# An attention and top-8 feed-forward kernel: the work after the last attention block rebuilt

## The chip, the cores and the metric

The kernel runs on one core of a Trainium2 chip. TensorE (PE) multiplies matrices, ScalarE (ACT) applies functions, VectorE (DVE) and GpSimd (POOL) work element by element, and SyncE (SP) issues the DMAs. The metric is the device time of one execution in microseconds; lower is better.

## What is computed

x is 2048 tokens by 448 features. With LN for a layer norm without weights:

```
h  = x + MHA(LN(x))        # 16 heads of 28, one shared K and V, softmax over all 2048 tokens
n  = LN(h)
r  = n @ w_r               # one score per token
idx = the 8 tokens with the largest r
y  = (silu(n[idx] @ w_gate) * (n[idx] @ w_up)) @ w_down * sigmoid(r[idx])
out = h + n, and y added to the 8 rows idx
```

w_gate and w_up are 448 x 1792, w_down is 1792 x 448. So 2040 of the 2048 rows of the output are known as soon as h is; only eight wait for the feed-forward part.

## The kernel before

**Blocks.** After a head that normalises x (16 tiles of 128 tokens) and makes K, V and Q, the attention runs as 16 blocks. Block b takes four heads (g = b % 4) and 512 queries (b // 4). For each of 16 key tiles PE makes scores into PSUM (`qk`, L593), either ACT turns 1024 of them into weights with Exp (`act_unit`, L601) or DVE does it with integer arithmetic (`dve_unit` L614, three `shift` L620), and PE multiplies with V into an accumulator bank, 6 or 7 (`act_pv`, `dve_pv`). Each block's accumulator holds four heads; one row per head is the row sum of the softmax.

**Row sums.** `post_block` (L499) copies the accumulator to SBUF (Ot, L506; on ACT for block 15), and then sends the row sums through DRAM: Ot's four sum rows to a scratch (L509), the scratch spread over 128 partitions into Lc (L510), DVE takes minimum and maximum for a flag and the reciprocal (L511 to L515), Lc goes back to the scratch (L516), and one row is read by 32 partitions each into Rb (L517). POOL multiplies Ot by Rb into On (L518). After every fourth block `out_proj` (L524) projects the four On for each of four token tiles, adds x, takes the layer norm's statistics, and writes outf (h + n, in place of x), xn (n) and the router score r (a weighted sum, L567, and a correction, L570). For blocks 3, 7 and 11 this runs beside the next block; for block 15 nothing runs beside it.

**After block 15.** The scores of all 16 tiles are transposed by PE, copied, sent by a DMA into one row of 2048 (L716), and DVE finds the eight largest and their places (L718, L719). A dozen small DVE steps split places and weights into bf16 parts, PE spreads them over the partitions (L736, L739), DVE makes a one-hot matrix oh (L743) and its transpose ohT (L746). PE gathers the eight rows of xn by 64 matmuls with oh (L749), then runs gate and up (56 matmuls each, L756), ACT and DVE form silu(g) * u * weight (L758 to L765), and 14 matmuls of 448 columns give y (L768). Then PE adds y into all 16 output tiles (L777: ohT as the stationary operand, and the identity times outf for every second tile), ACT or DVE copies each to ofin, and four DMAs of 448 KB store the output (L788).

**Order.** Nothing of this is scheduled by a compiler. Every step is recorded with a planned duration and a priority (`G.op`), and `plan` (L79) walks through a simulated time and gives each engine a fixed order: at each moment the ready step of lowest priority goes, and where only steps of a high priority are ready, they go early. Priorities are 16 per block: `at(16 * b + ...)`. At run time every engine follows its list strictly and waits on semaphores. So a step whose input comes later than planned holds all that stands behind it on its engine.

A second program in the kernel recomputes everything in a safer way if the flag says that a row sum left its range; it isn't run on these inputs.

## Time and profile before

| | |
|---|---|
| three runs | 473.23 us median (472.95 to 475.53) |
| the profiled execution | 475.65 us, its span 473.9 us |
| mean granted clock of TensorE | 0.924 |
| busy in the span | PE 365.2 us, PE weight loads 111.1, DVE 372.3, ACT 385.8, POOL 47.1 |
| instructions | 7880 |

The span runs from the first to the last instruction of the profiled execution. ACT is busy for 81% of it, but not evenly: it is nearly full until the last block ends at about 407 us, and then mostly idle.

### The profile page before, as it was taken

To read this page: it belongs to the slowest core of one execution; us is meant where nothing else is said; L and a number is where in the kernel's file an instruction comes from. 1 tells how busy PE (TensorE), PEld (TensorE's weight loads), DVE (VectorE), ACT (ScalarE), POOL (GpSimd) and SP (SyncE) were. 2 spreads that over 40 slices of the span, in tenths; PEclk is the share of its full clock that TensorE was granted. 3 is DMA by queue.
4 is the path that set the end of the run, shared out by engine and by line. 5 is a ranking of instruction groups with operands and counts; after the bars stand their busy time and mean duration, and the time that the engine had idled before them with its cause. 6 is when DMAs were issued, how large, how long until landed. Compare 5 with 4: busy or idle time off the path is not lost.

```text
span 473.9 us, 7880 instructions
## 1 busy us (share of the span) xinstructions
PE 365.2 (77%) x3228; PEld 111.1 (23%) x3228; DVE 372.3 (79%) x783; ACT 385.8 (81%) x430; POOL 47.1 (10%) x65
## 2 busy tenths in 40 slices
PE   1888798988879889888798888887988887240685
PEld 1333122222222222222222222221222222010630
DVE  5899469998968998999799899995898995046332
ACT  1488699999989999999899999997999999314012
POOL 8010001011011111010101010101020101310000
PEclk9988799999999999999999999998999999766565
DMA  8950000000000000000000000000000000000004
GB/s 220 254 163 10 0 25 3 24 3 25 2 24 1 23 4 26 3 24 1 24 3 24 3 24 3 23 5 24 1 25 3 23 3 24 3 21 1 1 8 154
DMA packets 15938, 14.62 MB, mean 31 GB/s; under 512 B 5960, under 2 KB 12888, under 8 KB 15896
## 3 DMA queue, kind: packets, MB, share of 16 engines
q1 hardware_dynamic: 15896, 14.05, 10.5%
q8 instruction: 27, 0.44, 0.4%
q14 instruction: 15, 0.12, 0.1%
HBM read 11.94 MB, written 2.10 MB: 30 GB/s over the span
## 4 chain that ended last, share of the span: by engine, by line
ACT 41%; DVE 24%; PE 22%; DMA 7%; issue 3%; POOL 2%; SPq 0%; POOLq 0%; DVEq 0%
ACT P L601 40%; PE ps L341 22%; DVE Y L614 8%; DVE Y L620 6%; DMA Rb<-l_scr 3%; DMA x_sb<-in_A_x_dram 1%; DVE Ot L506 1%; POOL On L518 1%; DVE K L481 1%; DVE bn L440 1%; DMA l_scr<-Lc 1%; DVE xnT L469 1%; DVE Vs L492 1%; PE ps L344 1%; DVE xn L455 1%
## 5 line engine op out<-in xcount | busy, mean ns | idle before, releaser
L601 ACT ACTIVATE P<-ps 128x1024 bf16<-128x1024 f32 x398 | 370.0, 1094 | 20.5 <-PE ps L341 19.1
L341 PE MATMUL ps<-Q,K 64*128 64x512 bf16 x1024 | 186.6, 391 | 48.4 <-ACT P L601 31.2
L614 DVE TENSOR_SCALAR Y<-ps 128x512 int16<-128x512 f32 x228 | 146.9, 681 | 21.5 <-PE ps L341 21.1
L620 DVE TENSOR_SCALAR Y<-Y 128x2048 int16<-128x2048 int16 x171 | 118.4, 731 | 1.6
L341 PEld LDWEIGHTS ps<-Q,K 64*128 64x128 bf16 x1024 | 45.0, 93 | 196.5 <-ACT P L601 147.9
L341 PE MATMUL ps<-P,Vs 128*32 128x512 bf16 x796 | 80.6, 395 | 0.7 <-ACT P L601 0.7
L341 PE MATMUL ps<-Y,Vs 128*32 128x512 bf16 x912 | 72.2, 381 | 0.0
L518 POOL TENSOR_TENSOR On<-Ot,Rb 128x512 bf16<-128x512 f32 x16 | 22.3, 1391 | 298.9 <-DMA Rb<-l_scr 298.9
L341 PEld LDWEIGHTS ps<-P,Vs 128*32 128x32 bf16 x796 | 20.5, 93 | 53.0 <-issue 51.1
L341 PE MATMUL ps<-wo_pad,On 128*128 128x448 bf16 x64 | 17.9, 399 | 12.7 <-POOL On L518 12.7
L341 PEld LDWEIGHTS ps<-Y,Vs 128*32 128x32 bf16 x912 | 23.1, 96 | 17.0 <-issue 7.2
L341 PE MATMUL ps<-xnT,wq_pad 112*128 112x512 bf16 x64 | 21.4, 430 | 2.9 <-DVE Ot L506 2.7
L534 DVE TENSOR_TENSOR hbuf<-ps,x_sb 128x448 f32<-128x448 f32 x16 | 9.9, 621 | 15.6 <-PE ps L341 15.6
L344 PE MATMUL ps<-ident,xn 128*112 128x128 bf16 x64 | 6.8, 271 | 12.2 <-POOL vone L397 10.6
L432 DVE TENSOR_SCALAR Q<-ps,qone 128x512 bf16<-128x512 f32 x16 | 11.6, 727 | 5.7 <-PE ps L341 5.6
L782 ACT ACTIVATE xnT<-ps 128x448 bf16<-128x448 f32 x8 | 4.3, 543 | 13.0 <-PE ps L341 13.0
L511 DVE TENSOR_TENSOR Lmn<-Lmn,Lc 128x16 f32<-128x16 f32 x16 | 2.7, 169 | 14.5 <-DMA Lc<-l_scr 14.5
L506 DVE COPY Ot<-ps 128x512 f32<-128x512 f32 x15 | 10.3, 684 | 4.9 <-PE ps L341 4.7
L541 ACT ACTIVATE st<-st 128x1 f32<-128x1 f32 x4 | 0.8, 190 | 16.1 <-DVE st L538 16.1
L546 POOL TENSOR_TENSOR st<-st,nhalf 128x1 f32<-128x1 f32 x12 | 8.3, 692 | 47.5 <-DVE st L538 47.5
L440 DVE BATCH_NORM_STATS2 bn<-x_sb 128x6 f32<-128x448 bf16 x16 | 9.4, 604 | 4.4 <-DMA x_sb<-in_A_x_dram 4.4
L758 ACT ACTIVATE eg<-ps 128x112 f32<-128x112 f32 x1 | 0.3, 263 | 13.4 <-PE ps L341 13.4
(122 smaller groups left out, 190.8 us busy)
## 6 DMA issues: line engine op xcount, KB each, us to landing
Rb<-l_scr SPq DMA_DIRECT2D x16, 256.0 KB
out_dram<-xnT SPq DMA_DIRECT2D x4, 448.0 KB, 3.2
wg_sb<-in_B_w_gate_dram SPq DMA_DIRECT2D x1, 1568.0 KB, 12.7
wu_sb<-in_B_w_up_dram SPq DMA_DIRECT2D x1, 1568.0 KB, 18.5
wd_sb<-in_B_w_down_dram SPq DMA_DIRECT2D x1, 1568.0 KB, 22.2
x_sb<-in_A_x_dram SPq DMA_DIRECT2D x3, 448.0 KB, 6.5
x_sb<-in_A_x_dram SPq DMA_DIRECT2D x2, 224.0 KB, 2.8
wq_sb<-in_A_wq_dram SPq DMA_DIRECT2D x1, 392.0 KB, 5.3
```

The source lines that it names most:

```text
L341: return lambda e: e.matmul(o, lhsT=l, rhs=r, start=start, stop=stop)
L344: return lambda e: e.transpose(o, i, ident[0:p, 0:p])
L432: G.op(DV, lambda e: e.tensor_scalar(Q[:, b % 4, :], ps[:, bank, :], qone[:, 0:1], None, ALU.add), dvt(512), reads=[pk(bank), "qone"], wri ...
L440: G.op(DV, [lambda e, t=t: e.bn_stats(bn6[:, t, :], x_sb[:, t, :])], dvt(D), reads=[("x", t)], writes=[("bn6", t)])
L455: G.op(DV, lambda e, t=t: e.tensor_scalar(xn[:, t, :], x_sb[:, t, :], mv[:, t, 0:1], rstd[:, t:t + 1], ALU.subtract, ALU.mult), 340, reads ...
L506: (lambda e: e.tensor_copy(Ot[:, rb, :], ps[:, acc_bank(b), :])), dvt(512), reads=[pk(acc_bank(b))],
L518: G.op(PO, lambda e: e.tensor_tensor(On[:, qb % 2, g, :], Ot[:, rb, :], Rb[:, rb, :], ALU.mult), 1270, reads=[("Ot", rb), ("Rb", rb)], wri ...
L534: G.op(DV, lambda e: e.tensor_tensor(hbuf[:, hr, :], ps[:, bank, 0:D], x_sb[:, t, :], ALU.add), dvt(D), reads=[pk(bank), ("x", t)], writes ...
L546: G.op(PO, lambda e: e.tensor_tensor(st[:, t, 4:5], st[:, t, 7:8], nhalf[:, 0:1], ALU.pow), 570, reads=[("st7", t), "nhalf"], writes=[("st ...
L601: G.op(AC, lambda e: e.activation(P[:, sl, :, :], ps[:, b0:b0 + 2, :], ACT.Exp, bias=EBIAS, scale=OCT), 905, reads=[pk(b0), pk(b0 + 1)], w ...
L614: G.op(DV, lambda e, k=k: e.tensor_scalar(Y[:, n, 0, p + 2 * k, :].bitcast(I16), ps[:, 4 + k, :], 0.0, 32639.0 - 3 * STEP, ALU.max, ALU.mi ...
L620: G.op(DV, lambda e: e.tensor_scalar(Y[:, n, v, :, :].bitcast(I16), Y[:, n, 0, :, :].bitcast(I16), v * STEP, None, ALU.add), 610, reads=[( ...
```

## The change

Everything up to the end of block 15 keeps its arithmetic; some work is put into it, and what comes after is rebuilt.

- **Row sums of block 15** take no DRAM trip: DVE clamps the accumulator into Ot in two halves, a matmul with a 0/1 matrix `sel` in fp32 spreads each head's sum over its 32 partitions, ACT takes Exp(-Ln), and DVE multiplies the accumulator by it in four quarters. The DMAs to Lc stay, for the flag alone.
- **Last four token tiles**: three of the four projection matmuls and the addition of x (by the identity) are issued before block 15 ends (`last_pre`, 16 matmuls), one each is left (`last_proj`). Statistics are taken straight from PSUM. The router score no longer needs the 448-wide sum after the norm: two more columns of `wo_pad` hold wo @ w_r (as a high and a low part) and xw holds x @ w_r, both worked out by DVE ahead of time (`last_w`, 8 wide sums at priority 40).
- **Router in two stages**: the 12 tiles known by block 13 are ranked during block 14 (`first_top`, `first_max`), their top eight rows are fetched by two indirect DMAs from POOL during block 15 (`second_top`); at the end only 8 + 512 scores are ranked, read by DVE from PSUM.
- **Stores**: after blocks 3, 7 and 11 SP stores 512 output rows and, to a scratch, 512 rows of xn (448 KB each). The last 512 output rows go as soon as they exist.
- **Feed-forward**: the eight rows are gathered by 20 matmuls with 128 stationary columns instead of 64 with 112. silu uses ACT (Exp, Ln, Exp) instead of a reciprocal on DVE. The down projection has w_down stationary: 56 matmuls with 8 moving columns on top of 20 that bring the rows of outf; PE transposes the result, DVE copies it, and POOL writes the eight final rows by one indirect DMA, which waits for all the stores.
- x_sb's rows grow from 448 to 452 columns, wo_pad's from 448 to 450; POOL sets up some small tables in the head; x_sb, xn and wd_sb get 16 spare columns at their ends, so that a slice of 128 columns never runs out. A step of POOL that overwrites what an earlier step of POOL reads now waits for it.

The diff, cut to its core:

```diff
+        if last:
+            G.prio = u - 30
+            for h in range(2):
+                c = slice(256 * h, 256 * h + 256)
+                G.op(DV, lambda e, c=c: e.tensor_scalar(Ot[:, rb, c], ps[:, acc_bank(b), c], LO / 4, HI * 4, ALU.max,
...
+                G.op(PE, mm(ps[:, 1, c], sel[:, :], Ot[:, rb, c], True, True), 450, reads=["sel", ("OtH", h)],
+                G.op(AC, lambda e, c=c: e.activation(Rb[:, rb, c], ps[:, 1, c], ACT.Ln), 270, reads=[pk(1)],
+                G.op(AC, lambda e, c=c: e.activation(Rb[:, rb, c], Rb[:, rb, c], ACT.Exp, scale=-1.0), 270,
...
+                    G.op(DV, lambda e, q=q: e.tensor_tensor(On[:, qb % 2, g, q], ps[:, acc_bank(b), q], Rb[:, rb, q],
+                                                            ALU.mult), 200,
+                         reads=[pk(acc_bank(b)), ("RbH", h)], writes=[("OnQ", k)])
...
+        if not last:
+            G.op(DV, lambda e: e.reciprocal(Lc[:, rb, :], Lc[:, rb, :]), 200, reads=[("Lc", rb)], writes=[("Lc", rb)])
+            dma(scr[b, 1].rearrange("i (r k) -> (i r) k", k=16), Lc[:, rb, :], [("scr1", b)], reads=[("Lc", rb)])
+            dma(Rb[:, rb, :], scr[b, 1].unsqueeze(1).broadcast_to([4, 32, 512]), [("Rb", rb)], reads=[("scr1", b)])
+            G.op(PO, lambda e: e.tensor_tensor(On[:, qb % 2, g, :], Ot[:, rb, :], Rb[:, rb, :], ALU.mult), 1270,
+                 reads=[("Ot", rb), ("Rb", rb)], writes=[("On", qb % 2, g)])
...
+        if k == 3:
+            evs.append(dma(out_v[:, t - 3:t + 1, :], outf[:, t - 3:t + 1, :], [("out", qb)],
+                           reads=[("outf", i) for i in range(t - 3, t + 1)]))
+            dma(xs[(t - 3) * 128:(t + 1) * 128, :].rearrange("(n p) d -> p n d", p=128), xn[:, t - 3:t + 1, :],
+                [("xs", qb)], reads=[("xn", i) for i in range(t - 3, t + 1)])
...
+        G.op(PE, mm(ps[0:12, bank, 0:128], x_sb[:, 0:12, D + 2], ident[:, :], True, True), 200,
+        G.op(DV, lambda e: e.tensor_copy(r12[:, :], ps[0:12, bank, 0:128]), 200, reads=[pk(bank)], writes=["r12"])
+        for c in range(3):
+            dma(r_row[0:1, 512 * c:512 * c + 512].rearrange("o (t p) -> o t p", p=128), r12[4 * c:4 * c + 4, :],
+                [("r_row", c)] + (old if c == 0 else []), reads=["r12"] + (old if c else []))
...
+        G.op(DV, lambda e: e.max(top8[:, 0, :], r_row[:, :]), 1700, reads=[("r_row", c) for c in range(3)],
+        G.op(DV, lambda e: e.max_index(idx8[:, 0, :], top8[:, 0, :], r_row[:, :]), 1760,
...
+        G.op(PE, mm(ps[0:8, bank, 0:1], posf[:, 0, :], ones1[:, 0:1], True, True), 100, reads=["ones1", ("posf", 0)],
+        G.op(DV, lambda e: e.tensor_scalar(idc[:, :], ps[0:8, bank, 0:1], 0.0, 1535.0, ALU.max, ALU.min), 70, reads=[pk(bank)], writes=["idc"])
+        G.op(DV, lambda e: e.tensor_copy(extc[:, D:D + 2], idb[:, :]), 70, reads=["idb0", "idb1"] + old,
...
+        for src, dst, nm, rd in ((out[0, 0:1536, :], extc, "extc", "out"), (xs, xnc, "xnc", "xs")):
+            G.op(PO, lambda e, src=src, dst=dst: e.indirect_dma_start(
+                dst[:, 0:D], None, src, bass.IndirectOffsetOnAxis(ap=idc[:, 0:1], axis=0)), 1000, dma=True,
+                reads=["idc"] + old + [(rd, q) for q in range(3)], writes=[nm])
...
+    def last_w():
+        for g in range(4):
+            G.op(DV, lambda e, g=g: e.scalar_tensor_tensor(junk[:, :], wo_pad[:, g, 0:D], 1.0, w_rb[:, :],
+                                                           ALU.mult, ALU.mult, accum_out=wor[:, g:g + 1]), 600,
+                 reads=["wo_pad", "w_rb"], writes=["junk", ("wor", g)])
...
+            G.op(DV, lambda e, k=k: e.scalar_tensor_tensor(junk[:, :], x_sb[:, 12 + k, 0:D], 1.0, w_rb[:, :],
+                                                           ALU.mult, ALU.mult, accum_out=xw[:, k:k + 1]), 600,
...
+        fns = [mm(ps[:, bank, 0:D + 2], On[:, 1, g, k * 128:(k + 1) * 128], wo_pad[:, g, :], g == 0, False)
+               for g in range(3)] + [mm(ps[:, bank, 0:D], ident[:, :], x_sb[:, t, 0:D], False, False)]
...
+        G.op(PE, mm(ps[:, bank, 0:D + 2], On[:, 1, 3, k * 128:(k + 1) * 128], wo_pad[:, 3, :], False, True), 200,
+        G.op(DV, lambda e: e.bn_stats(bn6[:, t, :], ps[:, bank, 0:D]), dvt(D), reads=[pk(bank)], writes=[("bn6", t)])
+        G.op(DV, lambda e: e.bn_aggr(mv[:, t, :], bn6[:, t, :]), 95, reads=[("bn6", t)], writes=[("mv", t)])
+        G.op(AC, lambda e: e.activation(st[:, t, 7:8], mv[:, t, 1:2], ACT.Ln, bias=EPS), 200,
+        G.op(AC, lambda e: e.activation(st[:, t, 4:5], st[:, t, 7:8], ACT.Exp, scale=-0.5), 200,
+        G.op(DV, lambda e: e.tensor_scalar(ra[:, k, 0:1], ps[:, bank, D:D + 1], ps[:, bank, D + 1:D + 2],
+                                           xw[:, k:k + 1], ALU.add, ALU.add), 85,
...
+        G.op(AC, lambda e: e.activation(xn[:, t, :], ps[:, bank, 0:D], ACT.Identity, bias=st[:, t, 6:7],
+                                        scale=st[:, t, 4:5]), 650,
+             reads=[pk(bank), ("st4", t), ("st6", t), ("st4", 15)], writes=[("xn", t)], prio=u + 20)
...
+            G.op(AC, lambda e: e.activation(outf[:, t, :], ps[:, bank, 0:D], ACT.Identity, bias=st[:, t, 6:7],
+                                            scale=st[:, t, 5:6]), 650,
+                 reads=[pk(bank), ("st5", t), ("st6", t), ("st4", 15)], writes=[("outf", t)])
...
+            G.op(DV, lambda e: e.tensor_scalar(outf[:, t, :], ps[:, bank, 0:D], st[:, t, 5:6], st[:, t, 6:7],
+                                               ALU.mult, ALU.add), 540,
+                 reads=[pk(bank), ("st5", t), ("st6", t), "oh5"], writes=[("outf", t)])
+        if k % 2:
+            evs.append(dma(out_v[:, t - 1:t + 1, :], outf[:, t - 1:t + 1, :], [("out", 3, k)],
+                           reads=[("outf", i) for i in range(t - 1, t + 1)]))
...
+                    at(16 * b + (14.6 if k < 3 else 17.0) + 0.1 * k, last_pre, k)
+                    at(16 * b + 20.0 + k, last_proj, k)
+    at(16 * 11 + 36.0, first_top)
+    at(16 * 14 + 4.0, first_max)
+    at(16 * 15 + 2.0, second_top)
+    at(16 * 2 + 8.0, last_w)
...
+        G.op(PE, mm(ps[0:1, 3, k * 128:(k + 1) * 128], x_sb[:, 12 + k, D + 2:D + 3], ident[:, :], True, True), 100,
+    G.op(DV, lambda e: e.max(top8[:, 1, :], row), 620, reads=[pk(2), pk(3)], writes=[("top8", 1)])
+    G.op(DV, lambda e: e.max_index(idx8[:, 1, :], top8[:, 1, :], row), 700, reads=[pk(2), pk(3), ("top8", 1)],
+    G.op(PE, mm(ps[:, 1, 0:8], ones1[:, :], posf[:, 1, :], True, True), 100, reads=["ones1", ("posf", 1)],
...
+        oh5[:, :, :], iota_n[:, :].unsqueeze(2).broadcast_to([128, 5, 8]),
+        ps[:, 1, 0:8].unsqueeze(1).broadcast_to([128, 5, 8]), ALU.is_equal), 150, reads=["iota_n", pk(1)],
+        writes=["oh5"])
...
+            fns.append(mm(psg[:, ch, :], xn_raw[:, o:o + 128], oh5[:, k, :], k == 0, False))
+        fns.append(mm(psg[:, ch, :], xnc[:, ch * CK:ch * CK + 128], oh5[0:8, 4, :], False, True))
...
+            fns.append(mm(psy[:, ch, :], x_raw[:, o:o + 128], oh5[:, k, :], k == 0, False))
+        fns.append(mm(psy[:, ch, :], extc[:, ch * CK:ch * CK + 128], oh5[0:8, 4, :], False, False))
+    G.op(AC, lambda e: e.activation(eg[:, :, :], pg[:, :, :], ACT.Exp, scale=-1.0), 170, reads=[pk(2)], writes=["eg"])
+    G.op(AC, lambda e: e.activation(eg[:, :, :], eg[:, :, :], ACT.Ln, bias=1.0), 170, reads=["eg"], writes=["eg"])
+    G.op(AC, lambda e: e.activation(eg[:, :, :], eg[:, :, :], ACT.Exp, scale=-1.0), 170, reads=["eg"], writes=["eg"])
-    G.op(PE, [mm(ps[0:8, 3, 0:D], guT[:, fc, :], wd_sb[:, fc, :], fc == 0, fc == NFC - 1) for fc in range(NFC)], 4800,
-         reads=["guT", "wd_sb"], writes=[pk(3)])
-    G.op(DV, lambda e: e.tensor_copy(yp[:, :], ps[0:8, 3, 0:D]), 600, reads=[pk(3)], writes=["yp"])
-        if on_act:
-            fns.append(mm(ps[:, bk, 0:D], ident[:, :], outf[:, t, :], False, True))
-        G.op(PE, fns, 230 * len(fns), reads=["ohT", "yp", "ident", ("outf", t)], writes=[pk(bk)])
-        if on_act:
...
-            evs.append(dma(out_v[:, t - 3:t + 1, :], ofin[:, t - 3:t + 1, :], [("out", t)],
...
+    G.op(PE, [mm(psy[:, ch, :], wd_raw[:, fc * D + ch * CK:fc * D + ch * CK + 128], guT[:, fc, :], False,
+                 fc == NFC - 1) for ch in range(NCH) for fc in range(NFC)], 1500,
+    G.op(PE, [mm(ps[0:8, 2, ch * CK:(ch + 1) * CK], yT[0:CK, ch, :], ident[0:CK, 0:CK], True, True)
+              for ch in range(NCH)], 400, reads=["yT", "ident"], writes=[pk(2)])
+    G.op(DV, lambda e: e.tensor_copy(fin[:, :], ps[0:8, 2, 0:D]), dvt(D), reads=[pk(2)], writes=["fin", "wq_sb"])
+    o = G.op(PO, lambda e: e.indirect_dma_start(out[0], bass.IndirectOffsetOnAxis(ap=idxc[:, 0:1], axis=0),
+                                                fin[:, :], None), 1000, dma=True,
+             reads=["fin", "idxc"] + [("out", q) for q in range(3)] + [("out", 3, 1), ("out", 3, 3)],
```

## Rows read from the trace of the kernel before

**Rows 1.** The page's chain of work that ended last, by engine, shares of the span.

```profile
ACT 41%; DVE 24%; PE 22%; DMA 7%; issue 3%; POOL 2%; SPq 0%; POOLq 0%; DVEq 0%
```

**Rows 2.** Windows by stage: PE, PEld, DVE, ACT, POOL busy (xcount), PEclk, DMA, GB/s.

```profile
64.00:404.00 340.00, 289.13 (x2638) 78.87 (x2638) 299.16 (x580) 331.28 (x359) 29.30 (x27) 0.99 0.05 14
407.40:419.50 12.10, 0.19 (x2) 0.09 (x2) 1.16 (x9) 0.60 (x1) 3.91 (x3) 0.57 0.08 24
419.50:431.80 12.30, 4.76 (x16) 1.92 (x16) 8.91 (x36) 6.27 (x16) 0.00 (x0) 0.78 0.00 0
431.80:442.30 10.50, 0.75 (x8) 0.38 (x8) 7.99 (x20) 0.77 (x2) 0.00 (x0) 0.50 0.00 1
442.30:448.80 6.50, 6.13 (x64) 6.07 (x65) 0.19 (x1) 0.00 (x0) 0.00 (x0) 0.50 0.01 3
448.80:452.90 4.10, 3.12 (x112) 3.05 (x112) 1.89 (x5) 0.26 (x1) 0.00 (x0) 0.50 0.02 4
452.90:458.40 5.50, 4.74 (x15) 1.59 (x15) 0.61 (x1) 0.00 (x0) 0.00 (x0) 0.64 0.00 0
458.40:473.90 15.50, 9.54 (x24) 1.81 (x24) 4.90 (x8) 4.34 (x8) 0.00 (x0) 0.56 0.37 123
```

**Rows 3.** Timeline of ACT: start us, us, instruction, idle before it and its releaser.

```profile
329.69 2.10 ACT L601 ACTIVATE P<-ps 128x1024 bf16<-128x1024 f32 x2 [3.21 <-PE ps L341]
407.44 0.60 ACT L505 ACTIVATE Ot<-ps 128x512 f32<-128x512 f32 x1 [0.57 <-PE ps L341]
```

**Rows 4.** Timeline of POOL: the row-sum products of blocks 11 and 14.

```profile
325.69 1.68 POOL L518 TENSOR_TENSOR On<-Ot,Rb 128x512 bf16<-128x512 f32 x1 [21.73 <-DMA Rb<-l_scr]
398.50 1.27 POOL L518 TENSOR_TENSOR On<-Ot,Rb 128x512 bf16<-128x512 f32 x1 [21.39 <-DMA Rb<-l_scr]
```

**Rows 5.** Timeline of DVE: blocks 1 and 2, and the end of block 15.

```profile
59.96 0.69 DVE L506 COPY Ot<-ps 128x512 f32<-128x512 f32 x1 [4.74 <-PE ps L341]
71.57 2.98 DVE L620 TENSOR_SCALAR Y<-Y 128x2048 int16<-128x2048 int16 x3
...
396.12 1.90 DVE L620 TENSOR_SCALAR Y<-Y 128x2048 int16<-128x2048 int16 x3
411.33 0.17 DVE L511 TENSOR_TENSOR Lmn<-Lmn,Lc 128x16 f32<-128x16 f32 x1 [13.32 <-DMA Lc<-l_scr]
```

**Rows 6.** Timeline of PE: the fp32 matmul of the flag (one in the code).

```profile
412.31 0.19 PE L341 MATMUL ps<-ones,bad 128*1 128x1 f32 x2 [4.99 <-DVE bad L702]
```

**Rows 7.** Groups by form: out<-in shapes xcount | busy us, mean ns | idle before.

```profile
L341 PE MATMUL ps<-oh,xn 128*112 128x8 bf16 x64 | 6.1, 234 | 1.5 <-DVE oh L743 1.5
L341 PE MATMUL ps<-xselT,wg_sb 112*128 112x8 bf16 x56 | 1.6, 168 | 0.4 <-DVE xselT L752 0.4
L341 PE MATMUL ps<-wd_sb,guT 128*8 128x448 bf16 x14 | 4.7, 518 | 1.0 <-DVE guT L765 1.0
L567 DVE SCALAR_TENSOR_TENSOR junk<-hbuf,st,w_rb 128x448 bf16<-128x448 f32 x16 | 10.9, 678 | 0.0
L536 DVE BATCH_NORM_STATS2 bn<-hbuf 128x6 f32<-128x448 f32 x16 | 10.0, 624 | 0.1
L554 ACT ACTIVATE x_sb<-hbuf,st 128x448 bf16<-128x448 f32 x4 | 3.0, 756 | 1.3 <-DVE st L550 1.2
L718 DVE MAX8 top<-Y 1x8 f32<-1x2048 f32 x1 | 2.3, 2283 | 1.9 <-DMA Y<-r 1.9
L758 ACT ACTIVATE eg<-ps 128x112 f32<-128x112 f32 x1 | 0.3, 263 | 13.4 <-PE ps L341 13.4
L763 DVE TENSOR_TENSOR sg<-ps,sg 128x112 f32<-128x112 f32 x1 | 0.3, 274 | 0.0
```

**Rows 8.** Chain of waits in order of time, one small DVE step: start, us, what.

```profile
425.33 0.07 DVE st L550
```

**Rows 9.** Issue to landing, us min/median/max: the four output stores, then the row-sum DMAs.

```profile
DMA to landing us min/median/max: 2.8/3.2/4.8
...
DMA to landing us min/median/max: 1.4/1.5/2.5
```

More of the change, by code (lines that the diff above doesn't have):

```diff
@@ L574, in _main @@
+    out_v = out[0].rearrange("(n p) d -> p n d", p=128)
+    evs = []
     groups = [4] * NB
@@ L657, in _main @@
             chunk(c)
+        last_w()
         nx = 0
@@ L772, in _main @@
[L772 to L789 removed]
+    G.prio = 310
@@ L790, in _main @@
+    evs.append(o)
     G.close(evs, "flag")
```

382 lines of the change are left out of this document (222 added, 160 removed).

## The prediction

> **What bounds the kernel now.** I read the chain of waits by engine first: ACT holds 41% of it, DVE 24%, PE 22% [rows 1], so there is more than one limit. The windows by stage say where each holds. From 64 to 404 us ACT is busy for 331.28 of 340 us, at a granted clock of 0.99 [rows 2]: the attention is bound by ACT's Exp, and PE (289.13) and DVE (299.16) run beside it with some 51 and 41 us to spare, about 3 us in each of its fifteen blocks. At 407.44 ACT takes the last accumulator [rows 3], and from there 66.5 us run to the end of the span, in which no engine is full over more than one stage. This tail is a chain of single steps: row sums 12.1 us, projection and norm 12.3, router 10.5, gather 6.5, gate and up 4.1, down 5.5, output 15.5 [rows 2]. What is taken off this chain comes off the time; what is put into the attention costs only what ACT loses by it.
>
> **The tail, part by part.** Times are worked out as the length of the new chain in each stage, with 0.03 to 0.05 us for each hop between engines.
>
> Row sums: four DMAs one behind the other and POOL's product go. In their place DVE clamps 256 columns: between 0.274 us for 112 and 0.624 for 448 [rows 7] that is 0.42. PE spreads them in fp32: one fp32 matmul shows as two records [rows 6], so two passes; 448 columns take 4.7 / 14 = 0.34 us [rows 7], 256 columns twice 0.39, with the drain 0.5 (bounds: one pass 0.3, four passes 0.9). ACT takes Ln and Exp, between 0.263 at 112 columns and 0.60 at 512 [rows 3, 7] 0.38 each. DVE multiplies the first quarter, 0.29. With hops 2.15 us; the second half follows beside the projection. Saved: 9.95.
>
> Projection and norm: one matmul a tile, 0.5 with its drain. DVE then does four statistics (0.624, some 0.54 apart) and about twenty one-column steps at 0.07 [rows 7, 8], 3.6 us, and after the last statistics a chain of aggregate, Ln, Exp and score, 0.9. The adds of x, the wide router sums (0.678 each [rows 7]) and ACT's 0.756 us outputs ahead of the last tile's Ln are gone from the path. 5.05 instead of 12.3; saved 7.25 (bounds 4 and 7 us for the stage).
>
> Router: PE's transposes 0.3; the maximum of 520 scores, 2.283 x 520 / 2048 = 0.58 [rows 7] and 0.1 of fixed time, 0.69; the search the same and 0.08; a cast, a spreading matmul and a one-hot of 40 columns 0.6; 0.3 until ACT's fourth xn (4 x 0.756 after the last Exp) is there. 2.7, where 10.5 held a DMA and two searches of 2.28. Saved 7.8. The new search reads PSUM, which no row shows; if it paid the full row's price, 3.2 more.
>
> Gather: 64 matmuls with 112 stationary columns took 6.1 us, 0.096 each; 56 with 128 took 1.6, 0.029 each [rows 7]. The new 20 have 128 columns, so I take 0.029: 0.6, with drain, copy and hops 1.1. Saved 5.4 (at 0.096 it would be 4.1).
>
> Gate and up stay at 3.12; the 20 matmuls that bring outf add 0.6 behind them, and silu (three ACT steps at 0.263 and three DVE steps at 0.274 [rows 7]) fits beside up and these. 3.75 instead of 4.1; saved 0.35.
>
> Down: 56 x 0.029 = 1.65, a copy 0.2, four transposes 0.4, a copy of 448 columns 0.62, hops: 3.05 instead of 5.5. Saved 2.45 (at 0.096 each it would be 1.3 us slower than now).
>
> Output: 24 matmuls, 16 copies and four stores in 15.5 us become one store of eight rows. No row shows an indirect DMA. Below, it is a small DMA: 1.5 us [rows 9]; above, the slowest store, 4.8 [rows 9], and two POOL steps of 1.27 [rows 4] and hops to make descriptors, 8. I take 3.0, a small DMA and one POOL step, since the data are small, and 0.5 to the end. Saved 12.0. What it waits for is earlier: the last two stores leave about when the router ends, eight microseconds before. The Trainium skill, page "DMA: Bandwidth & Descriptors", section "Anatomy of one DMA — SWDGE (gpsimd) path", gives about 2.0 us as the fixed price; by that the sum would be 1 us lower.
>
> Together 45.2 us: the tail would take 21.3 instead of 66.5.
>
> **What the attention pays.** (1) `last_w` and the head. It takes eight sums of 0.678 us and more. Four, those with wo, wait for four DMAs that the planner now thinks 14 us long each; they fall into block 2, where DVE has its share of spare time. The other four, with x, are ready early and fill every gap that the planner sees while K and Q are still being made; each then delays DVE by up to its length. DVE sits idle 4.74 us ahead of 59.96 [rows 5], so not all of it counts: 0.8 for both, with POOL's dozen set-up steps (bounds 0 and 6). (2) Router, first stage: 1.7 + 1.8 us of searches, a copy and some small steps, 4.5 us on DVE in blocks 13 to 15. DVE's last work in the attention ends at 398.02 and its next starts at 411.33, after 13.32 idle [rows 5], so it can be 9 us late at the end; what counts is PE held by DVE: 0.8 (bounds 0 and 4.5). (3) `last_pre` waits on PE for On of block 14, which POOL gives at 399.8 [rows 4]. PE's list is strict: if the planner puts it earlier, the scores behind it wait, and ACT with them. That is what happens now behind On of block 11: POOL works from 325.69, and ACT then idles 3.21 us [rows 3, 4]. POOL's two indirect loads stand before On of block 14, so a late index delays it further. I take 2.0 (bounds 0 and 3.2, and 2 more because 16 x 0.34 = 5.4 us of matmuls meet about 3 us of spare PE). (4) The six early transfers of 448 KB cost nothing: DMA is 0.05 busy [rows 2], and the row sums that queue behind them on SP, up to 4.8 us late [rows 9], are wanted three blocks later; if that cover went, On would be late by as much. (5) POOL's new waits cost nothing, POOL being busy for 29 of 340 us. A new order might also remove a stall, at best 3.2 [rows 3]. Sum 3.6, between -3 and 14.
>
> **The number.** 45.2 - 3.6 = 41.6. The profiled execution took 475.65 us (span 473.9), so 434.05 by its own time. It stands 2.42 above the median of the runs, 473.23; the forecast for the median is 431.6, written 432. A measurement of this kernel can tell 0.5%, 2.4 us, from no change.
>
> **Rivals.** *The attention pays in full* (chance 0.17): the sums at their upper prices, some 14 us instead of 3.6, 442 to 443. For it: PE and DVE have no more than 3 us spare in a block, and a strict order hands every delay on. Against it: ACT idles only now and then today. DVE and POOL also hold each other: three shifts take 2.98 us where POOL works beside them and 1.90 where it doesn't [rows 5], 1.08 for each meeting, twice for the two indirect loads. The Trainium skill, page "SBUF — State Buffer", section "SBUF: two separate sides", says that a DMA from POOL cannot have its descriptors written while DVE runs in a two-port mode. By that rule the loads in block 15 are late, not the last store, which has no DVE work beside it.
>
> *The indirect store is slow* (0.12): 8 us instead of 3, 437. For it: nothing in the trace bounds it well.
>
> *The clock rises* (0.08): the 208 matmuls with eight moving columns from gather to down run at 0.029 us; at twice the clock 3.0 us go, 429. Against it: from 442.3 to 452.9 PE was busy for 6.13 of 6.5 and 3.12 of 4.1 us, and the granted clock stayed at 0.50, the 1.2 GHz level [rows 2]. The Trainium skill, page "TensorE: Matmul & The Clock Gate", section "Loop structure matters more than you think", has matmuls that follow each other closely keep the engine fast. By that rule it would be 429; the rows of this stage disagree.
>
> *The stationary slices load slowly* (0.04): they start at multiples of 112 columns, not 128. 96 matmuls at 0.096 instead of 0.029 cost 6.4, 438.
>
> *Slower* (0.03): every list is planned anew, and if PE's held a stall like that of 3.21 us [rows 3] in each of the fifteen blocks that follow the head, 48 us would go, 480. It decides from 13 stalls on (41.6 / 3.21). Against it: ten blocks, 3 to 12, get no new work on PE, ACT or DVE.
>
> **Chances.** Forecast 0.56, the rivals 0.44. The range goes from 426 (clock up or a store of 1.5 us, and 1 to 2 us less in the attention) to 443, which takes in all but the last rival and the far ends. Faster by over 0.5%: 0.97; within: 0.01; slower: 0.02.
>
> **What would show it.** In the changed profile: about 2 us from the last accumulation to the first last projection, and no DMA there; two PE records for each half's fp32 matmul; searches of 0.7 us; gather and down at 0.03 us a matmul with the clock at 0.50; one store from POOL some 3 us before the end; ACT's last Exp 3 to 4 us later than now, with a gap of about 2 us ahead of it that PE's wait for On ends. I am wrong if ACT's last Exp ends over 7 us later, or the stretch behind it is not 18 to 26 us long.

## The result, and the profile after

The changed kernel takes 443.48 us (median of 4 runs, 439.79 to 446.67) against 473.09 for the kernel before beside it; the ratio is 0.9352, 95% interval 0.9261 to 0.9443. The profiled execution took 442.73 us, its span is 441.3. The forecast was 432, range 426 to 443. The direction was right; the gain is 29.6 us where 41 was forecast, and the median lies 0.5 us above the upper end of the range. One of the four executions, 446.67, was in a slower state; the median of the other three is 442.73.

Runs of one kernel here lie up to 7 us apart, so what follows is read stage by stage from the traces, and medians only decide what is larger than that. An Exp below is one of ACT's instructions that make softmax weights. The chain of waits by engine, after (answers to [rows 1]):

```profile
DVE 31%; ACT 29%; PE 25%; DMA 9%; POOL 2%; issue 1%; SPq 1%; POOLq 0%; DVEq 0%
```

ACT no longer leads. The windows by stage, after (answers to [rows 2]; the columns are the same): the attention, then row sums, projection and norm, router, gather, gate and up, down, output.

```profile
64.00:404.00 340.00, 289.39 (x2605) 78.02 (x2603) 304.46 (x605) 326.71 (x353) 31.52 (x29) 0.99 0.07 22
414.34:416.77 2.43, 1.44 (x5) 0.60 (x5) 1.10 (x4) 0.84 (x3) 0.00 (x0) 1.00 0.01 3
416.77:423.38 6.61, 1.92 (x8) 0.62 (x8) 5.53 (x34) 4.38 (x14) 0.00 (x0) 0.66 0.01 1
423.38:426.44 3.06, 1.04 (x5) 0.68 (x6) 2.61 (x16) 1.76 (x4) 0.00 (x0) 0.50 0.13 45
426.44:428.47 2.03, 2.03 (x28) 1.82 (x28) 1.63 (x4) 0.00 (x0) 0.00 (x0) 0.50 0.17 54
428.47:432.71 4.24, 4.24 (x133) 4.11 (x132) 1.04 (x5) 0.86 (x3) 0.00 (x0) 0.50 0.18 60
432.71:435.83 3.12, 2.19 (x61) 1.84 (x60) 0.80 (x2) 0.00 (x0) 0.00 (x0) 0.50 0.01 3
435.83:441.30 5.47, 0.00 (x0) 0.00 (x0) 0.01 (x1) 0.00 (x0) 0.93 (x1) 0.50 0.04 10
```

The tail is 26.96 us instead of 66.5; 21.3 was forecast. The last accumulation is read at 414.34 instead of 407.44: the attention pays 6.9, not 3.6. Where ACT lost it shows in its timeline (start, us, instruction, idle before it and its releaser), blocks 14 and 15:

```profile
362.76 2.85 ACT L753 ACTIVATE P<-ps 128x1024 bf16<-128x1024 f32 x3 [0.66 <-PE ps L349]
366.66 1.94 ACT L753 ACTIVATE P<-ps 128x1024 bf16<-128x1024 f32 x2 [1.04 <-PE ps L349]
...
403.45 1.02 ACT L753 ACTIVATE P<-ps 128x1024 bf16<-128x1024 f32 x1 [2.48 <-PE ps L349]
404.96 1.02 ACT L753 ACTIVATE P<-ps 128x1024 bf16<-128x1024 f32 x1 [0.49 <-PE ps L349]
406.52 6.88 ACT L753 ACTIVATE P<-ps 128x1024 bf16<-128x1024 f32 x7 [0.53 <-PE ps L349]
```

The first two stand behind the router's searches, the other three behind On of block 14. The chain of waits in order of time says why PE was late there (start, us, what):

```profile
395.15 5.03 DMA Rb<-l_scr
400.26 1.63 POOL On L563
401.93 12.39 PE ps L349 x89
```

The spread reciprocals took 5.03 us to land. The planner counts 2.0 for that DMA, so it put `last_pre`'s matmuls into PE's list some 3 us too early, and all scores behind them waited.

A ledger of ACT, from the windows of its Exps alone:

| | before | after |
|---|---|---|
| busy up to 110 us | 81.88 | 80.50 |
| idle from 110 us to the last Exp | 8.72 | 13.17 |
| last Exp ends | 406.87 | 413.40 |
| accumulation read | 407.44 | 414.34 |

The head (up to 110 us) gives 1.4 of the 6.9, which a later run shows to be within its scatter; waits behind it give 4.45; the other 1.05 are the hand-over (0.94 instead of 0.57) and Exps 0.7 longer in sum. Of the 4.45, 3.5 are the wait for On of block 14 and 1.9 the searches; the three old waits behind blocks 3, 7 and 11 came out 0.9 shorter.

### The profile page after: what moved, and what is told of

Same layout as the page of the kernel before. It is cut to its first block, busy times and chain, and to the rows that moved or that the text cites. A ratio compares the mean times of both kernels' runs of the same rounds, so it can differ in the third digit from the quotient of the medians.

```text
span 441.3 us, 7932 instructions
## 1 busy us (share of the span) xinstructions
PE 357.1 (81%) x3243; PEld 106.7 (24%) x3243; DVE 366.5 (83%) x792; ACT 382.1 (87%) x425; POOL 46.8 (11%) x76
## 4 chain that ended last, share of the span: by engine, by line
DVE 31%; ACT 29%; PE 25%; DMA 9%; POOL 2%; issue 1%; SPq 1%; POOLq 0%; DVEq 0%
ACT P L753 29%; PE ps L349 25%; DVE Y L766 11%; DVE Y L772 8%; DMA Rb<-l_scr 5%; DVE Ot L551 2%; DMA xnT<-r 2%; POOL On L563 1%; DMA x_sb<-in_A_x_dram 1%; DMA l_scr<-Lc 1%; DVE xn L479 1%; DVE bn L464 1%; DVE K L505 1%; DVE xnT L493 1%; DVE Vs L516 1%
## 5 line engine op out<-in xcount | busy, mean ns | idle before, releaser
L349 PE MATMUL ps<-Y,Vs 128*32 128x512 bf16 x912 | 75.2, 387 | 0.5 <-DVE Y L772 0.3
L349 PEld LDWEIGHTS ps<-Y,Vs 128*32 128x32 bf16 x912 | 22.7, 96 | 22.8 <-issue 11.5
L349 PE MATMUL ps<-wo_pad,On 128*128 128x448 bf16 (+1 forms) x64 | 18.0, 378 | 8.5 <-POOL On L563 7.7
L579 DVE TENSOR_TENSOR hbuf<-ps,x_sb 128x448 f32<-128x448 f32 x12 | 7.4, 619 | 4.6 <-PE ps L349 4.5
L349 PEld LDWEIGHTS ps<-wo_pad,On 128*128 128x128 bf16 x64 | 4.7, 100 | 17.7 <-POOL On L563 8.8
L352 PEld LDWEIGHTS ps<-ident,xn 128*112 128x112 bf16 x64 | 5.2, 161 | 13.3 <-POOL vone L405 10.6
L598 DVE SCALAR_TENSOR_TENSOR junk<-hbuf,st,w_rb 128x448 bf16<-128x448 f32 x12 | 8.1, 677 | 0.0
L349 PEld LDWEIGHTS ps<-xnT,wq_pad 112*128 112x128 bf16 x64 | 4.4, 104 | 14.7 <-DVE Ot L551 7.0
```

Of the source, the lines that this page charges most:

```text
L349: return lambda e: e.matmul(o, lhsT=l, rhs=r, start=start, stop=stop)
L352: return lambda e: e.transpose(o, i, ident[0:p, 0:p])
L579: G.op(DV, lambda e: e.tensor_tensor(hbuf[:, hr, :], ps[:, bank, 0:D], x_sb[:, t, 0:D], ALU.add), dvt(D), reads=[pk(bank), ("x", t)], writ ...
L598: G.op(DV, lambda e: e.scalar_tensor_tensor(junk[:, :], hbuf[:, hr, :], st[:, t, 4:5], w_rb[:, :], ALU.mult, ALU.mult, accum_out=st[:, t, ...
```

## The experiments

Theory: the attention pays because strict lists are written with landings that are too short, and the tail misses the forecast by single steps that can be named. Main rival: PE and DVE have too much work in blocks 13 to 15, and any wait taken away comes back elsewhere.

**The landing of Rb, in both kernels.**

```diff
-            dma(Rb[:, rb, :], scr[b, 1]..., [("Rb", rb)], reads=[("scr1", b)])
+            dma(Rb[:, rb, :], scr[b, 1]..., [("Rb", rb)], reads=[("scr1", b)], lat=5200.0)
```

> The changed kernel, with one number of its planner altered: the DMA that brings the spread reciprocals Rb is planned to land after 5.2 us, not 2.0 (its trace shows 5.03 us for block 15). Everything computed is the same. Theory A (part of the 6.9 us that the attention pays are waits on PE for On of blocks 3, 7, 11 and 14, because the list places those matmuls for an On that comes 3 us before it really does): the matmuls of last_pre stand some five Exps later in PE's list, the ACT gaps of 2.48 us at 403.45 and of 3.21 us at 237.04 go, the last accumulation is read at 406 to 409 us instead of 414.34, and the time is 6 to 9 us under that of the changed kernel: 435 to 438. Rival B (PE and DVE have simply too much work in blocks 13 to 15): the gaps turn up elsewhere, the last accumulation is read at 413 to 415 and the time is 442 to 445.

> The kernel before, with the same one number: Rb planned to land after 5.2 us. Theory A: the gaps of 1.93, 1.65 and 3.21 us behind blocks 3, 7 and 11 go (6.8 us together in its own trace), the last accumulation is read some 5 to 7 us earlier than 407.44, and the time is 466 to 468. Rival B: no change, 471 to 475. If it gains as much as the changed kernel does, the wait is old; what the change adds is then only the difference between the two gains, which A puts at 3 us for block 15's own wait.

The changed kernel takes 430.74 us with it (430.25 to 432.94), 12.7 less; the kernel before 463.23 (459.86 to 464.92), 8.8 less than the 472.02 beside it (ratio 0.9835, 0.9781 to 0.989). The accumulation is read at 402.19 and at 395.23, in both 12.2 us earlier, more than expected of either. Not all of that is the wait. ACT's idle time behind 110 us falls by 7.4 (13.17 to 5.79) and by 8.0 (8.72 to 0.68), its Exps take 2.0 and 1.6 less in sum, and 2.6 and 2.5 come from the head up to 110 us, where the lists with and without the edit are still the same: that part is scatter (below). So this one number of a planner is worth 7 to 8 us of waits, and 9 to 13 by medians that hold the scatter too. For the kernel before the rival falls: nothing of the wait comes back.

The attention still pays 6.96 (402.19 less 395.23), so the wait for On of block 14 was not all of it: in the changed kernel part of it did come back, as the rival has it. The timeline of the changed kernel with this edit, DVE and ACT in block 14:

```profile
350.88 1.75 DVE L629 MAX8 top<-xnT 1x8 f32<-1x1536 f32 x1 [4.49 <-DMA xnT<-r]
...
354.95 1.02 ACT L754 ACTIVATE P<-ps 128x1024 bf16<-128x1024 f32 x1 [4.20 <-PE ps L349]
```

DVE idled 4.49 us for the first router row, which three small DMAs bring, each planned at 2.0 us. ACT lost 4.20 and another 0.92. On SP's queue the first of the three is issued at 341.71 us, right behind the two stores of 448 KB. The other two follow only at 348.52:

```profile
348.52 1.20 SPq L363 DMA_DIRECT2D xnT<-r  x2
```

The kernel makes them wait until the first has landed (`old` in their reads), so the row pays one landing after another. No run took the stores away or let the three DMAs go at once, so what each of the two costs isn't told apart.

**The landing of the router row**, on top of that.

```diff
-                [("r_row", c)] + (old if c == 0 else []), reads=["r12"] + (old if c else []))
+                [("r_row", c)] + (old if c == 0 else []), reads=["r12"] + (old if c else []), lat=7500.0)
```

> The kernel with Rb planned at 5.2 us, and the three DMAs that lay the first router row planned to land after 7.5 us, not 2.0. Everything computed is the same. In the kernel with Rb alone DVE idled 4.49 us ahead of the first search, for the row to land, and ACT then lost 4.20 and 0.92 us in block 14. Theory (a wait of the same kind: a strict list and a landing taken too short): DVE doesn't idle ahead of the search, ACT loses 0 to 2.5 us there instead of 5.1, the last accumulation is read at 398.5 to 400.5 instead of 402.19, and the time is 427 to 429. Rival (the searches themselves, twice 1.75 us in which DVE makes no Y, are the price): ACT loses 4 to 5 us all the same and the time stays at 430 to 431.5.

425.19 us (424.29 to 428.59), better than expected. ACT's Exps from 110 us to the last one (length, busy, then clock and DMA), changed kernel and this one:

```profile
110.00:413.40 303.40, 290.23 (x313) 0.98 0.07 23
```

```profile
110.00:396.20 286.20, 285.60 (x311) 1.00 0.08 24
```

The idle time is 0.60 us instead of 13.17, as small as the 0.68 of the kernel before with its own wait taken away. The searches, twice 1.7 us on DVE, then cost nothing: what they cost depends on where they stand in the list and on how long they wait for the row. In the changed kernel DVE waited 0.65 us for it and ACT lost 1.9, with Rb's landing alone 4.49 and 5.1. The accumulation is read at 396.93, 1.7 behind 395.23, and ACT's busy time up to 110 us differs by as much (82.67 against 84.41). So the rival falls for the changed kernel too.

**The searches left out**, in the changed kernel as it is (two memsets in their place).

> The changed kernel without the two searches of the first router stage: the eight best of the first twelve tiles are replaced by constants that never win, so only the last four tiles are routed. Theory (the two searches of 1.75 us in block 14 hold DVE's exponentials, PE waits for them and ACT loses 1.9 us): the gaps of 0.66, 1.04 and 0.16 us at 362 to 369 go and the last accumulation is read 1.5 to 2.5 us earlier. Rival (the wait for On of block 14 that follows takes up what is gained): the gaps go, but the last accumulation is read within 0.7 us of 414.34.

From 342 to 375 us ACT is busy for all 33.00 us, so the 1.9 go; the accumulation is read at 411.54, 2.8 earlier, the gaps behind On of block 14 being 2.6 this time. 436.37 us (434.96 to 438.22), 7.1 less, of which 2 are a shorter end (see the last store, below). The rival (the next wait takes the gain) falls.

**The sums of `last_w` left out.**

> The changed kernel without the eight sums of last_w: the two score columns of wo stay at zero and the four sums of x with the router's weights are set to zero, so the scores of the last four tiles lack these parts. Theory (the head and these sums cost 1.4 us: ACT has done 88 Exps at about 112.2 us against 110.81 before): the 88th Exp is done at 110.8 to 111.2, and the last accumulation is read 1 to 2 us earlier. Rival (they lie in gaps of DVE, and the later 88th Exp is a plan that came out otherwise): no change beyond 0.5 us at the 88th Exp.

The 88th Exp is done at 109.63 us instead of 112.44 and ACT is busy for 83.03 us up to 110, 2.5 more than after, but the accumulation comes only 0.63 earlier, and the time is 440.40. This doesn't tell what `last_w` costs: executions of lists that keep it and are the same up to block 13 show 80.50 (after), 81.20 (SP's store) and 82.53 (full rows), and with full rows the 88th Exp is done at 110.34. The scatter is as large as the effect. What scatters is the clock. Windows of PE, DVE and ACT in the head, the changed kernel and the one with both landings:

```profile
51.00:62.00 11.00, 10.23 (x44) 1.99 (x44) 1.44 (x2) 8.85 (x11) 0.00 (x0) 0.50 0.00 1
```

```profile
51.00:62.00 11.00, 8.00 (x60) 2.15 (x58) 2.72 (x8) 10.72 (x12) 0.00 (x0) 1.00 0.00 1
```

In the first the granted clock is 0.50, the 1.2 GHz level, for 11 us; PE is busy for 10.23 of them and still late, and ACT gets 1.87 us less. PE had waited for DVE shortly before in both. The same decides how long a later wait is. In the kernel with two more set-up instructions (below) PE waits equally long for On behind block 3 and behind block 7; the first matmuls after the wait on PE, and ACT's next Exp:

```profile
137.77 1.68 PE L349 MATMUL ps<-wo_pad,On 128*128 128x448 bf16 x4 [1.57 <-POOL On L565]
140.03 1.02 ACT L755 ACTIVATE P<-ps 128x1024 bf16<-128x1024 f32 x1 [2.61 <-PE ps L349]
...
232.20 0.93 PE L349 MATMUL ps<-wo_pad,On 128*128 128x448 bf16 x4 [1.58 <-POOL On L565]
233.49 1.94 ACT L755 ACTIVATE P<-ps 128x1024 bf16<-128x1024 f32 x2 [1.65 <-PE ps L349]
```

Windows from PE's first matmul after the wait to ACT's next Exp:

```profile
137.75:140.05 2.30, 2.28 (x10) 0.65 (x10) 1.08 (x2) 0.02 (x1) 0.00 (x0) 0.50 0.00 0
232.20:233.50 1.30, 1.30 (x10) 0.50 (x10) 0.82 (x2) 0.01 (x1) 0.00 (x0) 1.00 0.00 0
```

The ten matmuls take 2.28 us at the granted clock of 0.50 and 1.30 at 1.00, and ACT's gap is 2.61 or 1.65 us. In the other traces it is the same: behind blocks 3, 7 and 11, where PE waited 1.57 us, the gap is 1.65 wherever the clock stayed and 2.45 to 2.61 wherever it fell. Of the 3.21 us behind block 7 in the changed kernel the clock is one part; there PE also waited 2.17.

**The end of the row sums, and ACT's order.** In the tail of the changed kernel the timeline shows two waits that the forecast lacks:

```profile
415.99 0.70 PE L349 MATMUL ps<-Ot,sel 128*128 128x256 f32 x2 [0.47 <-ACT Rb L539]
...
422.26 0.72 ACT L704 ACTIVATE xn<-ps,st 128x448 bf16<-128x448 f32 x1 [0.24 <-DVE st L701]
422.88 0.19 ACT L691 ACTIVATE st<-st 128x1 f32<-128x1 f32 x1
```

The second half's matmul writes the PSUM bank that ACT still reads, and xn of tile 14 stands ahead of the Exp that tile 15's score waits for: its read of that Exp is registered before the Exp exists, so nothing orders them.

```diff
-                G.op(PE, mm(ps[:, 1, c], sel[:, :], Ot[:, rb, c], True, True), ...
+                G.op(PE, mm(ps[:, 1 + 2 * h, c], sel[:, :], Ot[:, rb, c], True, True), ...
...
-        G.op(AC, lambda e: e.activation(xn[:, t, :], ...
+        for q in range(4 if k == 3 else 0):
+            last_xn(q)
```

> The changed kernel with two edits in the tail: the second half of the row sums goes into PSUM bank 3 instead of bank 1, and the four activations that make xn are registered behind all four last projections, so that ACT takes the Exp of tile 15 first. Everything computed is the same. Theory (the stage from the first last projection to the last transposed score took 6.61 us, not the forecast 5.05, because the second spreading matmul waits 0.47 us for ACT to read the same bank and xn of tile 14, 0.72 us, stands ahead of the Exp of tile 15): the second matmul starts at once, 0.7 to 0.8 us earlier, the last transpose comes 1.0 to 1.6 us earlier after the first read of the accumulator (9.04 us now, 7.4 to 8.0 then). Rival (DVE's four statistics and its one-column steps of 0.15 to 0.28 us are the bound): under 0.6 us gained.

From the read of the accumulator to the last transposed score 8.17 us instead of 9.04. 0.87 lies between theory and rival: both waits are gone. That DVE's chain of four statistics and its small steps bounds the rest is argued, not shown. The time is 438.49 us; 2 of the 5 us less are again a shorter end.

**The row sums by DMA again**, all else as changed.

> The changed kernel with the row sums of block 15 in the old way: DVE copies the accumulator, four DMAs carry the sums to DRAM and back, and the product is made by DVE in quarters when the spread reciprocals land. Everything computed is the same. Theory (the matmul and ACT's Ln and Exp take the place of 12.1 us by 2.43): from the read of the accumulator to the first last projection 11.5 to 13 us, and the time 9 to 10.5 us longer. Rival (part of the trip was waited for with other work that now has to be done anyway): 5 to 8 us longer.

11.10 us in that stage instead of 2.43, 8.7 more; 449.85 us, 6.4 more. The time hides 2.1 of it, because the end of this kernel was shorter, which the next two show; so the DRAM trip costs some 8.5 us. That lies between theory and rival. The time alone would have spoken for the rival.

**The last store.**

```diff
-    o = G.op(PO, lambda e: e.indirect_dma_start(out[0], bass.IndirectOffsetOnAxis(ap=idxc[:, 0:1], axis=0),
-                                                fin[:, :], None), 1000, dma=True,
+    o = G.op(SP, lambda e: e.dma_start(out[0, 0:8, :], fin[:, :]), 60, dma=True,
```

> The changed kernel, whose last store is a plain one of SP to rows 0 to 7 instead of the indirect one of POOL to the eight chosen rows; so eight rows are misplaced. Theory (the 5.42 us from the last copy of DVE to the end hold POOL's own price, 0.93 us for its DMA instruction and some 0.3 us ahead of it, and the rest is the landing): this stretch takes 3.8 to 4.5 us, 1.0 to 1.6 us less. Rival (the landing and the final wait are all of it): less than 0.5 us gained. Second rival (the indirect form costs far more than an issue, as in the forecast's rival of a slow store): over 2.5 us gained.

5.48 us from the last copy to the end, against 5.47. A plain store of the same eight rows saves nothing, so the indirect form is not what makes the end long. But five other kernels, whose store is unchanged, end in 3.17 to 3.41 us (the next expectation names them). One thing in which the two groups may differ is how the instruction lists are laid out, so the next edit only lengthens two of them:

```diff
+    G.op(DV, lambda e: e.memset(bad1[:, :], 0.0), 70, writes=["bad1"])
+    G.op(PO, lambda e: e.memset(top8[:, :, :], 0.0), 100, writes=[("top8", 0), ("top8", 1)])
```

> The changed kernel with two more set-up instructions that do nothing for the result, a memset of 128x1 on DVE and one of 1x16 on POOL, both in the head. Everything computed is the same. What it tests: from the end of DVE's last copy to the end of the span the changed kernel took 5.47 us, the one with SP's plain store 5.48, but those without last_w, without the first searches, with the second PSUM bank, with the row trip and with full rows 3.2 to 3.4, though the store is the same in all of these. Theory (the length of the instruction lists decides, since after the store has landed the cores of the two groups differ by a fetch of instructions whose end must be waited for or not): 3.2 to 3.4 us. Rival (what decides is in the edits themselves or in the store): 5.4 to 5.5 us. The time of the whole is 441 to 444 by the first, 442 to 446 by the second, and doesn't tell them apart.

3.42 us: two idle instructions in the head take 2.05 us off the end. Windows of the end, after and this one (the last two columns are DMA share and GB/s):

```profile
437.60:438.00 0.40, 0.00 (x0) 0.00 (x0) 0.00 (x0) 0.00 (x0) 0.00 (x0) 0.50 0.09 18
439.20:439.60 0.40, 0.00 (x0) 0.00 (x0) 0.00 (x0) 0.00 (x0) 0.00 (x0) 0.50 0.27 61
439.60:441.30 1.70, 0.00 (x0) 0.00 (x0) 0.00 (x0) 0.00 (x0) 0.00 (x0) 0.50 0.00 0
```

```profile
432.80:433.20 0.40, 0.00 (x0) 0.00 (x0) 0.00 (x0) 0.00 (x0) 0.00 (x0) 0.50 0.09 18
434.00:434.50 0.50, 0.00 (x0) 0.00 (x0) 0.00 (x0) 0.00 (x0) 0.00 (x0) 0.50 0.11 33
```

In both the store's 7 KB go first and a burst follows 1.2 to 1.6 us later; in the changed kernel the span lasts 1.7 us beyond it, in the other it ends with it. The long ends (after, Rb alone, both landings, SP's store: 5.31 to 5.48) belong to kernels that fetched 27 and 15 packets of instructions on their two queues; those of 3.17 to 3.58 fetched one or two fewer. That it is a fetch of instructions which some engine waits for is thus possible, not shown. The number of instructions alone doesn't decide: kernels with fewer recorded than the changed one's 7932 (7916 without `last_w`) and with more (8094 with a warm PE) both have the short end. What is shown is that neither the form of the store nor the work in the tail makes it. The median of this kernel, 438.74, is 4.7 below the changed one, but its head was also at the better clock (83.56 busy up to 110 us).

**Eight fetched rows, widened to 128.**

```diff
-        fns.append(mm(psg[:, ch, :], xnc[:, ch * CK:ch * CK + 128], oh5[0:8, 4, :], False, True))
+        fns.append(mm(psg[:, ch, :], xncf[:, ch * CK:ch * CK + 128], oh5[:, 4, :], False, True))
```

> The changed kernel with the two tiles of fetched rows widened from 8 to 128 rows, the rows behind zero-filled by POOL in block 14, so that all 40 gathering matmuls have 128 rows. Everything computed is the same. The gather's 20 matmuls took 1.26 us, 0.063 each, and not 0.029 as forecast. Theory (each stationary slice of 8 rows breaks the stream: 0.10 us of weight load for it against 0.19 for four full ones, and the next four start anew): the 20 take 0.6 to 0.75 us, those of x the same, and the two stages together are 1.0 to 1.3 us shorter. Rival (a short group of matmuls costs that, whatever its rows, because the four slices come from places 448 columns apart): within 0.3 us of now.

Groups by form, after, then this one (count, busy us, mean ns):

```profile
L349 PE MATMUL ps<-oh,xnT 8*128 8x8 bf16 x8 | 1.5, 183 | 0.0
L349 PE MATMUL ps<-oh,x_sb 128*128 128x8 bf16 x16 | 1.1, 172 | 0.0
L349 PE MATMUL ps<-oh,xn 128*128 128x8 bf16 x16 | 1.1, 171 | 0.4 <-DVE oh L883 0.4
```

```profile
L349 PE MATMUL ps<-oh,xnT 128*128 128x8 bf16 x8 | 1.1, 168 | 0.0
L349 PE MATMUL ps<-oh,x_sb 128*128 128x8 bf16 x16 | 0.8, 169 | 0.1
L349 PE MATMUL ps<-oh,xn 128*128 128x8 bf16 x16 | 0.6, 168 | 0.4 <-DVE oh L884 0.4
```

The gather stage is 1.53 instead of 2.03, gate and up 3.82 instead of 4.24: 0.92 together, just under the 1.0 to 1.3 expected. One slice of 8 rows among four of 128 makes a group of five last 0.31 us; five of 128 rows start 0.13 apart from the next five. The Trainium skill, page "TensorE: Matmul & The Clock Gate", section "LDWEIGHTS (loading the stationary operand)", says that a load with few rows takes as long as one with 128; the trace of the changed kernel agrees, with 98 ns for a load of 8 rows and 102 to 119 for one of 128 in the gather. What the mix costs is overlap: the matmul of the 8-row slice starts 0.100 us after the one ahead of it, and the next one 0.115 after that, where slices of 128 rows follow each other in 0.027.

**All of it together**, with four small edits of the tail: statistics ahead of small steps, the overflow test later, all four last outputs on ACT, two spreading matmuls in fp16.

> All that helped, together: both planned landings, the second PSUM bank and the late xn, fetched rows widened to 128, and four more edits of the tail: the statistics ahead of older tiles' one-column steps, the order of the overflow test behind them, all four last outputs on ACT, and the two spreading matmuls with one row in fp16 instead of fp32. The eight weights are rounded to fp16 by this, nothing else. By the traces: the last accumulation is read at 398.5 to 400.5; the tail takes row sums 2.4, projection and norm 5.0 to 5.4 (6.61), router 2.6 to 2.8 (3.06), gather 1.1 to 1.3 (2.03), gate and up 3.7 to 3.9 (4.24), down 3.1, end 3.2 or 5.5: 21.3 to 24.0 in all, and the time is 421 to 426. Against the theory of waits speaks a time over 427; against the theory of the tail's single steps a tail over 24.5 us.

423.53 us (420.96 to 424.6), ratio 0.8957 (0.8897 to 0.9017). The tail is 22.62: row sums 2.50, projection and norm 5.62, router 2.73, gather 1.05, gate and up 4.04, down 3.10, output 3.58; 26.87 with both landings alone. But the profiled execution had the clock at 0.50 from 51 to 62 us, and the accumulation is read at 400.18, not 396.93, though nearly nothing in the lists up to there differs: scatter of the head hides 3.25 of the 4.25 us that the tail gains. By the medians the whole is 1.7 below the kernel with both landings.

**A warm PE in the tail.** 80 matmuls that nothing reads, where PE waits.

```diff
+    def warm(n, after):
+        G.op(PE, [mm(ps[:, 7, 0:128], ident[:, :], ident[:, :], True, True)] * n, 55 * n, reads=["ident", after],
+             writes=[pk(7)], prio=310.5)
+
+    warm(36, ("OnQ", 3))
+    warm(12, ("r", 13))
+    warm(32, ("r", 15))
```

> The kernel with all that helped, plus 80 matmuls of 128x128 that nothing reads (identity times identity into a bank that is free), in three blocks of 36, 12 and 32 where PE waits in the tail: behind the last projection, behind the second transposed score and behind the fourth. Everything else is the same. In the kernel without them the granted clock is 1.00 until 405 us and 0.50 from there to the end; PE had no work from 404 to 406.48, and the stages from gather to the last transposes take 1.05, 4.04 and 3.10 us. Theory (the clock falls because PE idles there, and the matmuls with eight columns would run faster at the upper level, the forecast's rival of a rising clock): the clock stays at 1.00 to the gather and beyond, gate and up take 2.2 to 2.8 us, down 2.0 to 2.4, and the tail is 2 to 3.5 us shorter: 420 to 421.5 us against 423.53. Rival 1 (the stream of eight columns doesn't hold the clock, whatever comes before it): 1.00 up to the gather and 0.50 again inside gate and up; the tail gains 0.3 to 1.2 us. Rival 2 (the added matmuls stand in the way of the transposes by more than they give): projection, norm and router take 0.5 to 2 us longer and the time is 423.5 to 425.5.

The gather on PE without them, its first and its last step (start, us, instruction):

```profile
411.03 0.24 PE L353 MATMUL ps<-oh,xn 128*128 128x8 bf16 x4 [0.45 <-issue]
411.54 0.17 PE L353 MATMUL ps<-oh,xnT 128*128 128x8 bf16 x1
```

With them, and then windows of PE (length, busy, clock, DMA share, GB/s) from the gather into gate:

```profile
411.77 0.24 PE L353 MATMUL ps<-oh,xn 128*128 128x8 bf16 x4 [0.34 <-issue]
412.25 0.17 PE L353 MATMUL ps<-oh,xnT 128*128 128x8 bf16 x1
```

```profile
411.70:412.50 0.80, 0.73 (x21) 1.00 0.00 0
...
413.00:413.50 0.50, 0.50 (x26) 0.66 0.97 335
413.50:414.00 0.50, 0.50 (x25) 0.50 0.30 100
```

The clock stays at 1.00 through the gather and falls inside gate, though PE is busy there without a gap. And it hardly matters: from the first to the last of the 20 matmuls of the gather, 19 steps, it takes 0.48 us at 1.00 and 0.51 at 0.50, so they start 0.025 and 0.027 us apart. The tail is 22.74, the time 422.52 (420.91 to 425.23), not to be told from 423.53. Theory and first rival are both wrong on the gain; the rival was right that the clock falls in gate. The Trainium skill, page "TensorE: Matmul & The Clock Gate", section "Wait — 56ns, not 53.3ns?", has two matmuls start never less than about 25 ns apart, however few columns; the trace agrees.

The medians in one place, with what each leaves out or alters told above:

| kernel | us |
|---|---|
| before, after | 473.09, 443.48 |
| before, with Rb's landing | 463.23 |
| after, with Rb's landing; with both landings | 430.74; 425.19 |
| no searches; no `last_w` | 436.37; 440.40 |
| second bank and late xn; full rows | 438.49; 438.54 |
| SP's store; row sums by DMA; two more instructions | 442.19; 449.85; 438.74 |
| all together; and a warm PE | 423.53; 422.52 |

The kernels without the searches or `last_w`, with the second bank, full rows, the row sums by DMA or two more instructions, and the last two have the short end; 2 us of what lies between them and the others is that.

## Why the prediction was right, and by how much it was off

The mechanisms were right: the tail is a chain of single steps that could be shortened step by step, and the attention pays through waits on PE in strict lists, at the place that the forecast named. The sizes were short, nearly all in the same direction. The forecast missed by 11.5: 3.3 in the attention and 5.7 in the tail. The other 2.5 are mostly the step to the median: 2.42 were taken off because the profiled execution of before lay above its median, and that of after lies 0.75 below its own; rounding and the time outside the span give 0.7 back. With executions up to 7 us apart it is chance on which side of 443 the median falls.

Of the two signs by which the forecast would call itself wrong, one came. ACT's last Exp ended 6.5 us later (413.40 against 406.87), within the 7 allowed. But the stretch behind it is 27.9 us long (413.40 to 441.30), not 18 to 26: by its own test the tail was sized too short.

- *Row sums*, 2.15: 2.43, and 8.7 saved by the run that undid it, 9.95 forecast. Right.
- *Projection and norm*, 5.05: 6.61. Mis-sized. The step "about twenty one-column steps at 0.07" took the smallest row [rows 8]; between the first statistics and the last small step DVE's 23 small steps start 0.04 to 0.20 us after one another, 0.11 in the mean, which is 0.9 more. 0.87 us are the two waits that the second bank and the late xn take away. Together that is 0.2 over the miss; the stage's other terms came out that much shorter.
- *Router*, 2.7: 3.06. The search reads PSUM at 0.69 us, as forecast; the excess is the fp32 spreading matmul, two records in 0.59.
- *Gather*, 1.1: 2.03. The price of 0.029 was right for a matmul of 128 rows behind another (they start 0.027 apart), and wrong for the four with 8 rows and for the one behind each. Five matmuls for the row numbers and the fp32 spread of the weights, 0.59, which PE runs ahead of gate, weren't counted.
- *Gate and up*, 3.75: 4.24, the same 8 rows. *Down*, 3.05: 3.12, right; slices at multiples of 112 cost nothing, and that rival is gone.
- *Output*, 3.5: 5.47. The store itself was sized right: 0.93 us on POOL and 2.2 from issue to landing, 3.2 to 3.6 to the end in the kernels with a short end. 2 us are the end of the program, whose cause is open. The rival of a slow indirect store is wrong: a plain one takes as long.
- *Attention (1)*, `last_w` and the head, 0.8: 1.4, but the head scatters by as much with its clock; nothing is shown of `last_w`. *(2)*, searches, 0.8: 1.9 after, 5.1 with Rb's landing alone, 0 with both. *(3)*, On of block 14, 2.0: 3.5. The mechanism was right and named with its place; the size was short; the cause, a planned landing of 2.0 against 5.03, wasn't looked for. It stood in [rows 3, 4] for block 11 as well, and the same number held up the kernel before by some 8 us. *(4)*, early transfers, 0: not borne out in one point: the router row is issued right behind two of them, and in the list with Rb's landing DVE waited 4.49 us for it; the row's own DMAs, which wait for one another, are the other part. *(5)*, POOL, 0: nothing speaks against it; On of block 14 waited for the landing of Rb, not for POOL's indirect loads.
- *Rivals.* "The attention pays in full" was nearest in time, 442 to 443, but half of the miss is in the tail. (The upper bounds that it adds up give 15.7 us, not 14: 6, 4.5, 3.2 and 2.) That DVE and POOL would hold each other at the two indirect loads did not show: from 390.40 to 392.84 us DVE's shifts beside them took 0.67 to 0.69 each, as long as elsewhere. "The clock rises": it can be made to stay up to the gather, and gives nothing, so 429 was never there; the argument against it, from the clock in [rows 2], was right on the clock and silent on the price. A stall in every block did not come.
